# Attention and a gated feed-forward on one Trainium2 core: q loads on GpSimd's queue, a norm in small pieces, products and sums moved in chunk 1

## The chip, the cores and the metric

The kernel runs on one core of a Trainium2 chip. The core has five engines with instruction streams of their own: TensorE (PE in the profile; PEld is its loading of weights), VectorE (DVE), ScalarE (ACT), GpSimd (POOL) and SyncE (SP), which here only issues DMA transfers. ACT and GpSimd can issue transfers too. Every engine executes its stream in order and waits on semaphores for the others. The metric is the time of one execution on the device, in microseconds (us).

## What is computed

The reference, cut to what matters. The attention has no softmax, so k and v are first contracted to a 64 x 64 matrix for each head; every row of a head's output is normalised by its root mean square. The result, 4608 rows of 512, goes through a gated feed-forward layer. The weights come in 64-bit floats.

```python
# q, k, v: (8 batches, 8 heads, 576, 64)   w_gate, w_val: (512, 1536)   w_out: (1536, 512)
kv  = einsum('bhsd,bhse->bhde', k, v)
out = einsum('bhsd,bhde->bhse', q, kv)
rms = sqrt(mean(out * out, axis=-1, keepdims=True) + 1e-06)
x   = (out / rms * g_norm).transpose(0, 2, 1, 3).reshape(8 * 576, 512)
gate = 1 / (1 + exp(-(x @ w_gate)))
y    = (gate * (x @ w_val)) @ w_out
```

## The kernel before

**Chunks.** The feed-forward works in nine chunks of 512 rows. Chunk 0 is computed plainly (`Plain`, L592; `second`, L828). Chunks 1 to 8 use a fast scheme of matrix multiplication: sums of blocks of x, of the weights and of h are formed first, so that 26 block products do the work of 32 (`PRODUCTS1` for the first layer, `PRODUCTS2` for the second; `X_SUMS`, `SUMS` and `W_SUMS` list the sums). The first layer of a chunk, `first_layer_fast`, runs three blocks j = 0, 1, 2 of 26 products, so 78 places p = 0 to 77, about 0.86 us of PE each (L952). The second layer, `second_layer_fast`, runs 26 products over the three blocks (L1056).

**Attention beside it.** Batch 0 is done at the start (`attention`). The attention of batch b = 1 to 7 is cut into steps (`feed`) that are put between the matmuls of chunk b - 1, at places written out by hand: `places` for chunk 0, where a place is a matmul of 512 columns and runs from 0 to 87, and `where` for the later chunks, where it is p. A batch has two head runs, m = 0 and 1. The steps of one run are: two turns of q by VectorE (t, L402 and L404), the matmuls into a PSUM tile of three banks called `at` (u, L433), the square by ACT (q in `where`, L438), two sums by VectorE (s, L441), the root by ACT (r, L444), the norm (n) and two transposes back by VectorE with their stores to the x ring (x, L456 to L467). There is one `at` tile, so the second run's matmuls, and the next batch's key-value products (L387, L394), wait until the norm of the run before has read it. In batches 1 and 2 the norm is a reciprocal on VectorE (L477, L479) and 18 scalings by ACT (L473), one for every head slice; in the later batches VectorE does it.

**Loads.** `load_q_run(b, m)` brings a run's q in transposed order: 12 transfers, eight of 32 x 18 pieces of 128 bytes (L118) and four of 32 x 2 pieces (L119). All are issued by SP (`nc.sync`), in program order with the 24 + 12 halves of the weight units (`load_unit`, L160 and L162) and with k and v of the coming batch (`load_late`, L133 and L138). Batch 1's q goes into space of h that is not in use yet. A weight unit is 512 rows by 128 columns of w_gate and of w_val, converted from 64-bit words by five VectorE and two ACT instructions (`convert`: L196, L211, L223, L227, L234 on VectorE, L201 and L216 on ACT). Three units are staged at a time; the next load of a stage waits for VectorE's L227 of the unit that was in it.

**Fast products.** After product i of the first layer `combine` executes its steps: copies out of PSUM by ACT (L918), sums by VectorE (L922), sigmoids by ACT (L911), and products of the gate and the value (the steps with `*`, L914) by the engine that is given as `mult`. Five PSUM banks go round: a product that opens a region takes the bank that was freed longest ago, and `give_all` frees a region's bank after its last step. In a block's last product (K, i = 25) the regions H and K are open; the sums `o6=H+t8` and `o4=o4+K` release their banks. The products of h then feed the sums of h (`h_sums`, L726), which GpSimd makes, except eight that VectorE makes in the third block. GpSimd executes a block's sums one for each later product.

**Sums of weights.** The sums of w_gate and w_val are made once by GpSimd (`w1_sums`, L745), during chunk 0 and the start of chunk 1. The sums of w_out (`w_form`, L1027 and L1029) are made once, in chunk 1, at places listed for the first layer (`at1`) and the second (`at2`), each on GpSimd or on VectorE, as the third number says; each is stored to a scratch in device memory, from which later chunks load it.

Of the kernel before, what the change touches and what calls it, by code (L numbers as in the profile page):

```python
# [20 lines left out]
def kernel(  # L21
# [11 lines left out]
    nc = tc.nc  # L33

    B, H, S, HD = q.shape
# [69 lines left out]
    def load_q_run(b, m):  # L105
        if b >= B:
            return
        if b == 1:
            t = h_main[2 - m].rearrange("p s c -> p (s c)")[:, 4 * NT * P - QW:4 * NT * P]
        else:  # L110
            t = sb.tile([P, QW], FP32, tag="q", name="q", bufs=1)
        main = t[:, 0:2 * S].rearrange("p (e j c) -> p e j c", e=2, c=QB)
        more = t[:, 2 * S:QW].rearrange("p (e j c) -> p e j c", e=2, c=QB)
        for i in range(NC):
            for e in range(2):
                for g in range(2):
                    src = q[b, 4 * m + 2 * g + e].rearrange("(p j) d -> p j d", j=JR)[:, :, QB * i:QB * i + QB]
                    nc.sync.dma_start(out=main[HD * g + QB * i:HD * g + QB * i + QB, e], in_=src)  # L118
                nc.sync.dma_start(out=more[QB * i:QB * i + QB, e], in_=src[:, JR - 2:JR])  # L119
        q_late[b, m] = t  # L120

    kv_late = {}
# [251 lines left out]
    def feed(b):  # L374
# [35 lines left out]
        def heads_run(m):  # L410
# [57 lines left out]
                                                          in_=xTs[p0:p0 + QB, i, :, s0:s0 + n_])  # L468
                            s0 += n_

            def norm(r):
                for n in range(6 * r, 6 * r + 6):
                    nc.scalar.activation(out=by_head(sq)[:, n], in_=by_head(d["u"])[:, n], func=AF.Copy,  # L473
                                         scale=ms[:, n:n + 1])
# [12 lines left out]
        u0, u1 = heads_run(0), heads_run(1)  # L487
        if b == 1:
            return kv, t0 + t1 + u0 + u1, ()
        names = "t00 t01 t10 t11 u0 q0 s00 s01 r0 n00 n01 x00 x01 u1 q1 s10 s11 r1 n10 n11".split()  # L490
        steps_ = dict(zip(names, t0 + t1 + u0 + u1[:7]))
# [7 lines left out]
        return kv, first, u1[7:]  # L499

    def flush():
        while fill:
# [129 lines left out]
    for token in order.split():  # L632
# [13 lines left out]
        else:  # L646
            a[f][steps[name]]()
            if token == f"Q{NE - 1}":
# [29 lines left out]
    PRODUCTS2 = (("A", 8, 4, "o5=A"), ("C", 9, 1, "o4=C"), ("B", 18, 10, "o3=B"), ("A", 24, 14, "o1=A"),  # L678
# [253 lines left out]
    def first_layer_fast(c, at):  # L932
# [3 lines left out]
        for j in range(N3):  # L936
            o = {f"t{n}": pair(temps[:, i]) for i, n in enumerate((0, 1, 8, 9))}
            for n in (3, 1, 2, 0):
                o[f"o{n}"] = pair(sg_tile())
            h = h_main[j].rearrange("p (g e t) c -> p g e (t c)", g=2, e=2)  # L940
            for n in range(4):
                o[f"o{4 + n}"] = h[:, :, n // 2, GH * (n % 2):GH * (n % 2) + GH]
            regions = {}
            for i, (name, hv, wv, steps) in enumerate(PRODUCTS1):
                part, p = next(n for n, r in enumerate(PARTS) if i in r), NPR * j + i
                new = name not in regions
                if new:
                    i_ = free.popleft()
                    regions[name] = i_, pair(bank(i_))
                ws = w1_form(c, j, part, hv)  # L950
                for g in range(2):
                    nc.tensor.matmul(regions[name][1][:, g], ws[:, g], xf[c][wv], start=(new and g == 0), stop=True,  # L952
                                     skip_group_check=True)
                combine(o, regions, steps, nc.vector if i == NPR - 1 and (j == N3 - 1 or c == 1 and j == 1) else nc.gpsimd)
                give_all(regions, LAST1, i)
                for step in at.get(p, ()):
                    step()
                for _ in range(2 if i % HALF == HALF - 1 else 1):
                    if h_fill:
                        h_fill.popleft()[1]()  # L960
                if c > 1:
                    g_ = NPA * (N3 * (c - 2) + j) + part
                    if p < NPR * N3 - 1:
                        wait = (3 if part < 2 else 0) if j == 0 and c + 1 < B else 0
                        if wait and i == PARTS[part][-1]:
                            held[i + wait] = g_ + NPA
                        elif i == PARTS[part][-1]:
                            load_granule(g_ + NPA)
                        if j == 0 and i in held:
                            load_granule(held.pop(i))  # L970
                    if stores and p >= 24 and p % 2 == 0:
                        stores.popleft()()
                    k_, r = divmod(p - (38 if c == 2 else 20), 2)
                    if r == 0 and 0 <= k_ < NR:
                        load_w((c - 2) * NS + k_)
                else:
                    if p == 0:
# [151 lines left out]
    for c in range(1, NG):  # L1129
# [15 lines left out]
                else:  # L1145
                    x_late.append((p - NPR, step))
        if c == 1:
            for at_, forms in ((at1, ((28, 9, 0), (30, 10, 0), (34, 12, 0), (52, 8, 1), (56, 13, 0), (58, 14, 0), (64, 16, 1), (66, 11, 1), (74, 19, 0))), (at2, ((1, 22, 0), (3, 23, 1), (4, 25, 1), (9, 15, 0), (10, 24, 0), (10, 20, 0), (11, 17, 0), (12, 18, 0), (13, 21, 0)))):
                for p, n, pool_ in forms:
                    at_.setdefault(p, []).append(lambda n=n, eng=nc.gpsimd if pool_ else nc.vector, at_once=at_ is at1: w_form(n, eng, at_once))  # L1150
        first_layer_fast(c, at1)
        if c == 1:
            sgs += [spare_sg] + more_sgs
# [31 lines left out]
```

## Time and profile before

| what | value |
|---|---|
| time, median of 3 runs | 1014.05 us (1013.87 to 1014.34) |
| the profiled execution, its own time | 1011.93 us |
| its span, first to last instruction | 1010.2 us |
| mean granted TensorE clock | 0.998 |
| PE busy | 996.6 us, 99% |
| DVE busy | 720.6 us, 71% |
| POOL busy | 587.5 us, 58% |
| ACT busy | 341.7 us, 34% |
| transfers | 195.42 MB, mean 193 GB/s |

Three chunks in the chain of work that ended last, all by lines of PE: chunk 0 plain up to 162.72 us, chunk 1 from there to 270.92, and chunk 2 to 377.74. A chunk from the second to the sixth takes 106.6 us, of which 5.0 belong to the attention of the next batch; the last two, which have none beside them, take 101.0.

How to read it: all times are from the start of the span. "Busy" leaves out register, branch, semaphore and DMA-issuing instructions. Matmuls are pipelined and their ends are modelled, so PE's share of 99% hides stalls of some tenths of a microsecond; they are seen as gaps between the starts of matmuls. In the waits, "A <- B" means that engine A's instruction waited, and that B was what came last. SPq and POOLq stand for the instruction queues that issue transfers.

### The profile page before, as it was taken

The page shows a single profiled execution, that of the slowest core. Times are in us where ns is not written, and L with a number is a line of the kernel's source. Part 1 is how long each engine was busy: PE and PEld are TensorE (multiplying, and loading weights), DVE is VectorE, ACT ScalarE, POOL GpSimd, SP SyncE. Part 2 cuts the span into 40 slices and gives each one's busy share as a digit, 9 for nine tenths or more (in the row PEclk, how much of TensorE's full clock was granted, in tenths as well). Part 3 has the DMA queues.
Part 4 walks back from the last instruction along what each step waited for, and adds up shares of the span by engine and source line. Part 5 has one row for each costly group of instructions (what it writes and reads, how often), then busy time and mean ns, then how long its engine had stood idle before and what let it go on. Part 6 is the DMA issues. An engine that isn't in the chain of part 4 may idle for free.

```text
span 1010.2 us, 16595 instructions
## 1 busy us (share of the span) xinstructions
PE 996.6 (99%) x5958; PEld 819.5 (81%) x5958; DVE 720.6 (71%) x1201; ACT 341.7 (34%) x605; POOL 587.5 (58%) x961
## 2 busy tenths in 40 slices
PE   8999999999999999999999999999999999999998
PEld 7444446878888888888888888888888888888887
DVE  4968998889768847775667666866688556755672
ACT  4547432472134303441244114421352133213320
POOL 0000899896539651967187706962596449744963
PEclk9999999999999999999999999999999999999999
DMA  9887423664699569756776477756764545444514
GB/s 274 241 230 222 153 81 97 217 201 163 198 306 278 166 202 274 222 161 200 224 240 197 151 231 237 218 158 183 247 208 151 174 157 210 163 150 159 213 57 123
DMA packets 165201, 195.42 MB, mean 193 GB/s; under 512 B 94560, under 2 KB 138208, under 8 KB 165120
## 3 DMA queue, kind: packets, MB, share of 16 engines
q0 software_dynamic: 20976, 112.87, 32.7%
q1 hardware_dynamic: 136976, 79.40, 28.3%
q10 hardware_dynamic: 7168, 2.10, 0.9%
q8 instruction: 47, 0.77, 0.3%
q14 instruction: 34, 0.28, 0.1%
HBM read 160.50 MB, written 25.56 MB: 184 GB/s over the span
## 4 chain that ended last, share of the span: by engine, by line
PE 89%; SPq 3%; DVE 3%; DMA 3%; ACT 2%; issue 1%; POOL 0%; ACTq 0%; DVEq 0%; POOLq 0%
PE mm L952 52%; PE mm L1056 26%; PE mm L828 4%; SPq L118 2%; PE mm L592 2%; PE at L433 1%; DMA st<-in_moe_w_val_dram 1%; PE at L387 1%; SPq L119 1%; ACT sqs L473 1%; PE at L592 1%; DMA h_more<-in_v_dram 1%; DMA h_more<-in_k_dram 1%; PE mm L645 0%; DVE w L1029 0%
## 5 line engine op out<-in xcount | busy, mean ns | idle before, releaser
L952 PE MATMUL mm<-xs,w 128*128 128x256 f32 x1428 | 332.2, 380 | 0.6 <-DVE h L922 0.5
L952 PEld LDWEIGHTS mm<-xs,w 128*128 128x128 f32 x1428 | 271.1, 191 | 37.5 <-DVE h L922 0.9
L952 PE MATMUL mm<-xT,w 128*128 128x256 f32 x948 | 230.1, 380 | 0.5 <-ACT temps L918 0.5
L952 PEld LDWEIGHTS mm<-xT,w 128*128 128x128 f32 x948 | 180.0, 191 | 25.3 <-ACT temps L918 0.9
L922 DVE TENSOR_TENSOR sg<-sg,mm 128x512 f32<-128x512 f32 (+1 forms) x176 | 100.9, 600 | 86.6 <-PE mm L952 41.8
L774 POOL DMA_DIRECT2D w<-kept x84 | 46.9, 558 | 191.3 <-PE mm L952 189.0
L1056 PE MATMUL mm<-w,h 128*128 128x256 f32 x630 | 142.9, 380 | 0.0
L1056 PEld LDWEIGHTS mm<-w,h 128*128 128x128 f32 x630 | 120.0, 191 | 16.1 <-POOL h L726 0.2
L918 ACT COPY temps<-mm 128x512 f32<-128x512 f32 (+1 forms) x128 | 66.2, 539 | 188.1 <-PE mm L1056 94.7
L726 POOL TENSOR_TENSOR h<-h 128x128 f32<-128x128 f32 x216 | 113.3, 536 | 16.7 <-DVE h_more L726 13.2
L914 POOL TENSOR_TENSOR h<-h,sg 128x512 f32<-128x512 f32 x69 | 91.9, 1348 | 50.0 <-DVE h L922 30.0
L1056 PE MATMUL mm<-w,h_more 128*128 128x256 f32 x474 | 108.5, 380 | 0.7 <-DVE h L922 0.7
L911 ACT ACTIVATE sg<-sg 128x512 f32<-128x512 f32 x96 | 59.7, 630 | 134.5 <-DVE sg L922 134.5
L1056 PEld LDWEIGHTS mm<-w,h_more 128*128 128x128 f32 x474 | 90.3, 191 | 13.0 <-DVE h L922 1.1
L918 ACT COPY sg<-mm 128x512 f32<-128x512 f32 (+1 forms) x112 | 57.1, 511 | 87.4 <-PE mm L1056 48.1
L726 POOL TENSOR_TENSOR h_more<-h 128x128 f32<-128x128 f32 x120 | 62.6, 525 | 36.5 <-DVE h L914 32.2
L592 PE MATMUL mm<-xT,w 128*128 128x512 f32 x176 | 78.8, 602 | 0.9 <-DVE w L234 0.8
L922 DVE TENSOR_TENSOR temps<-temps,mm 128x512 f32<-128x512 f32 (+1 forms) x96 | 59.5, 620 | 26.5 <-PE mm L1056 17.2
L922 DVE TENSOR_TENSOR temps<-mm,temps 128x512 f32<-128x512 f32 (+1 forms) x64 | 39.8, 622 | 53.7 <-PE mm L1056 23.6
L918 ACT COPY h<-mm 128x512 f32<-128x512 f32 x48 | 28.2, 588 | 138.3 <-PE mm L952 124.8
L922 DVE TENSOR_TENSOR sg<-mm,sg 128x512 f32<-128x512 f32 (+1 forms) x64 | 39.7, 620 | 44.2 <-PE mm L952 23.5
L745 POOL TENSOR_TENSOR h_more<-w 128x256 f32<-128x256 f32 x10 | 10.6, 1074 | 101.9 <-DMA st<-in_moe_w_out_dram 101.9
(140 smaller groups left out, 1278.8 us busy)
## 6 DMA issues: line engine op xcount, KB each, us to landing
w<-kept POOLq DMA_DIRECT2D x42, 896.0 KB, 5.2
w<-kept POOLq DMA_DIRECT2D x90, 384.0 KB, 4.6
w<-kept POOLq DMA_DIRECT2D x42, 768.0 KB, 5.2
out_dram<-sg SPq DMA_DIRECT2D x119, 64.0 KB, 1.7
h_more<-in_k_dram SPq DMA_DIRECT2D x28, 256.0 KB, 5.3
h_more<-in_v_dram SPq DMA_DIRECT2D x28, 256.0 KB, 5.6
q<-in_q_dram SPq DMA_DIRECT2D x96, 72.0 KB, 5.1
xT<-xTs SPq DMA_DIRECT2D x96, 72.0 KB, 4.5
```

What stands on the lines that cost most here:

```text
L118: nc.sync.dma_start(out=main[HD * g + QB * i:HD * g + QB * i + QB, e], in_=src)
L592: nc.tensor.matmul(self.ps[i], w[("wg", "wv")[i], self.f][:, m, :], xT[self.c][:, m, :], start=(m == 0), stop=(m == NMT - 1), skip_group_c ...
L726: ops.append((eng, lambda v=v, x=x, sign=sign, y=y, eng=eng: eng.tensor_tensor(out=h_form(v, j), in0=h_form(x, j), in1=h_form(y, j), op=op ...
L745: nc.gpsimd.tensor_tensor(out=w1_slot(j, w_at[v]), in0=w1_slot(j, w_at[x]), in1=w1_slot(j, w_at[y]), op=op_of(sign))
L774: nc.gpsimd.dma_start(out=granule(g)[:, 0:n], in_=kept1[g // NPA % N3, g % NPA][:, 0:n])
L828: nc.tensor.matmul(ps[t], gv[0, f][:, P * t:P * t + P], w["wo", f], start=(f == 0), stop=(f == NFT - 1), skip_group_check=True)
L911: nc.scalar.activation(out=o["o" + step[1]], in_=o["o" + step[1]], func=AF.Sigmoid)
L914: mult.tensor_tensor(out=o[x], in0=o[x], in1=o[y], op=ALU.mult)
L918: nc.scalar.copy(out=o[out_], in_=o[expr])
L922: tt(out=o[out_], in0=o[x], in1=o[y], op=ALU.add if sign == "+" else ALU.subtract)
L952: nc.tensor.matmul(regions[name][1][:, g], ws[:, g], xf[c][wv], start=(new and g == 0), stop=True, skip_group_check=True)
L1056: nc.tensor.matmul(regions[name][1], h_form(hv, j), ws[:, j], start=(used[i] and j == 0), stop=(j == N3 - 1), skip_group_check=True)
```

## The change

Four edits.

1. `load_q_run` takes its queue by the batch: batch 1's 24 transfers are issued by GpSimd (`nc.gpsimd`), all others by SP as before. In the program they stand at places 2 and 11 of chunk 0, ahead of GpSimd's first sums of the weights (place 73).
2. Batch 2's norm, in chunk 1, was the reciprocal with six scalings, then twelve more; now it is the reciprocal as a step of its own and six steps of three scalings. The hand-written places are new: the first run's root moves from 42 to 35, its norm from 48 and 50 to 36 to 44, its transposes from 52 and 53 to 51 and 52; the second run's norm from 60 and 62 to 62 to 69.
3. In chunk 1's second block (j = 1) the three products of K's group go from VectorE to GpSimd. In all chunks and blocks the steps of that group are in a new order: the sum and the product of o7 first.
4. Form 13 of w_out, a sum on VectorE, moves from place 56 of chunk 1's first layer to the second finished product of its second layer; form 22 moves one product further there. Form 13 is still stored at once.

```diff
-                    nc.sync.dma_start(out=main[HD * g + QB * i:HD * g + QB * i + QB, e], in_=src)
-                nc.sync.dma_start(out=more[QB * i:QB * i + QB, e], in_=src[:, JR - 2:JR])
+        queue = nc.gpsimd if b == 1 else nc.sync
+                    queue.dma_start(out=main[HD * g + QB * i:HD * g + QB * i + QB, e], in_=src)
+                queue.dma_start(out=more[QB * i:QB * i + QB, e], in_=src[:, JR - 2:JR])
...
-            def norm(r):
-                for n in range(6 * r, 6 * r + 6):
+            def norm(r, per=6):
+                for n in range(per * r, per * r + per):
...
-                norms = [lambda: (nc.vector.reciprocal(ms, ms), norm(0)), lambda: (norm(1), norm(2))]
+                norms = [lambda: nc.vector.reciprocal(ms, ms)] + [lambda r=r: norm(r, 3) for r in range(6)]
...
-        where = """0:t00 5:t01 25:u0 26:q0 28:t10 30:s00,s01 33:t11 42:r0 48:n00 50:n01 52:x00 53:x01,u1
-                   56:q1 57:s10,s11 60:r1,n10 62:n11""" if b == 2 else """
+        where = """0:t00 5:t01 25:u0 26:q0 28:t10 30:s00,s01 33:t11 35:r0 36:n00 37:n01 39:n02 40:n03 42:n04 43:n05 44:n06
+                   51:x00 52:x01 53:u1 56:q1 57:s10,s11 60:r1 62:n10,n11 63:n12 65:n13 66:n14 68:n15 69:n16""" if b == 2 else """
...
-                 ("K", 43, 2, "o4=o4+K o7=o7-t8 o4*o0 o6=H+t8 o6*o2 o7*o3"))
+                 ("K", 43, 2, "o7=o7-t8 o7*o3 o4=o4+K o4*o0 o6=H+t8 o6*o2"))
...
-                combine(o, regions, steps, nc.vector if i == NPR - 1 and (j == N3 - 1 or c == 1 and j == 1) else nc.gpsimd)
+                combine(o, regions, steps, nc.vector if j == N3 - 1 and i == NPR - 1 else nc.gpsimd)
...
-            at1: (52, 8, 1), (56, 13, 0), (58, 14, 0) ...     at2: (1, 22, 0), (3, 23, 1) ...
+            at1: (52, 8, 1), (58, 14, 0) ...                  at2: (1, 13, 0), (2, 22, 0), (3, 23, 1) ...
-            at_once=at_ is at1
+            at_once=at_ is at1 or n == 13
```

More of the change, by code (lines that the diff above doesn't have):

```diff
@@ L489, in feed @@
             return kv, t0 + t1 + u0 + u1, ()
-        names = "t00 t01 t10 t11 u0 q0 s00 s01 r0 n00 n01 x00 x01 u1 q1 s10 s11 r1 n10 n11".split()
-        steps_ = dict(zip(names, t0 + t1 + u0 + u1[:7]))
-        where = """0:t00 5:t01 25:u0 26:q0 28:t10 30:s00,s01 33:t11 42:r0 48:n00 50:n01 52:x00 53:x01,u1
-                   56:q1 57:s10,s11 60:r1,n10 62:n11""" if b == 2 else """
+        n_ = "n{0}0 n{0}1 n{0}2 n{0}3 n{0}4 n{0}5 n{0}6" if b == 2 else "n{0}0 n{0}1"
+        names = f"t00 t01 t10 t11 u0 q0 s00 s01 r0 {n_.format(0)} x00 x01 u1 q1 s10 s11 r1 {n_.format(1)}".split()
+        steps_ = dict(zip(names, t0 + t1 + u0 + u1[:-2]))
+        where = """0:t00 5:t01 25:u0 26:q0 28:t10 30:s00,s01 33:t11 35:r0 36:n00 37:n01 39:n02 40:n03 42:n04 43:n05 44:n06
+                   51:x00 52:x01 53:u1 56:q1 57:s10,s11 60:r1 62:n10,n11 63:n12 65:n13 66:n14 68:n15 69:n16""" if b == 2 else """
                    5:t00 8:t01 28:u0 29:t10 30:q0 33:s00,s01 36:r0 39:t11 41:n00 47:n01 51:x00,x01 54:u1
@@ L498, in feed @@
         first = [(int(w_.split(":")[0]), steps_[x]) for w_ in where.split() for x in w_.split(":")[1].split(",")]
-        return kv, first, u1[7:]
+        return kv, first, u1[-2:]
     def flush():
@@ L1147 @@
         if c == 1:
-            for at_, forms in ((at1, ((28, 9, 0), (30, 10, 0), (34, 12, 0), (52, 8, 1), (56, 13, 0), (58, 14, 0), (64, 16, 1), (66, 11, 1), (74, 19, 0))), (at2, ((1, 22, 0), (3, 23, 1), (4, 25, 1), (9, 15, 0), (10, 24, 0), (10, 20, 0), (11, 17, 0), (12, 18, 0), (13, 21, 0)))):
+            for at_, forms in ((at1, ((28, 9, 0), (30, 10, 0), (34, 12, 0), (52, 8, 1), (58, 14, 0), (64, 16, 1), (66, 11, 1), (74, 19, 0))), (at2, ((1, 13, 0), (2, 22, 0), (3, 23, 1), (4, 25, 1), (9, 15, 0), (10, 24, 0), (10, 20, 0), (11, 17, 0), (12, 18, 0), (13, 21, 0)))):
                 for p, n, pool_ in forms:
-                    at_.setdefault(p, []).append(lambda n=n, eng=nc.gpsimd if pool_ else nc.vector, at_once=at_ is at1: w_form(n, eng, at_once))
+                    at_.setdefault(p, []).append(lambda n=n, eng=nc.gpsimd if pool_ else nc.vector, at_once=at_ is at1 or n == 13: w_form(n, eng, at_once))
         first_layer_fast(c, at1)
```

## The prediction

> **What bounds the kernel now.** I read, in this order: the page's shares, the waits of PE, the chain of waits that ended last, busy time by stretches, then the timelines around every stall. PE is busy 99% of the span, so only a stall of PE, or work that keeps PE waiting, is worth anything. The waits of PE (what waited, for what: us in total, times, longest) name the long ones:
>
> ```profile
> PE at L433 <- ACT sqs L473: 3.2, 2, 2.5
> PE mm L592 <- DVE w L234: 0.8, 1, 0.8
> ```
>
> The 2.5 us is one stall of chunk 0 at 75.7 us: the second head run of batch 1 needs the PSUM tile that the norm of the first (ACT, L473) still reads. The chain of waits (start, length, what) says why that norm is late:
>
> ```profile
> 53.48 1.38 SPq L118
> ...
> 58.19 4.41 DMA st<-in_moe_w_val_dram
> 62.62 0.70 DVE w L196
> ...
> 98.75 3.67 ACT sqs L473 x18
> ```
>
> SP issues batch 1's q in small pieces (L118) up to 58.2; only then can it issue the second half of weight unit 6, for which VectorE waits. The stretches (us, then busy time of PE, PEld, DVE, ACT, POOL, clock, DMA share, GB/s):
>
> ```profile
> 55.00:60.00 5.00, 5.00 (x13) 2.10 (x11) 0.81 (x2) 0.00 (x0) 0.00 (x0) 1.00 0.53 85
> 75.00:77.50 2.50, 0.73 (x2) 0.00 (x0) 0.48 (x2) 2.50 (x10) 0.00 (x0) 1.00 1.05 354
> 77.50:80.00 2.50, 1.73 (x68) 1.73 (x70) 2.46 (x3) 2.47 (x6) 0.00 (x0) 0.71 0.73 135
> 80.00:82.50 2.50, 2.50 (x15) 1.33 (x10) 2.50 (x7) 0.38 (x2) 0.00 (x0) 0.61 0.43 67
> 209.00:230.60 21.60, 19.54 (x152) 15.75 (x151) 18.58 (x26) 14.69 (x43) 20.95 (x29) 1.00 0.63 210
> ```
>
> While SP issues q, the transfers run at 85 GB/s where 354 is seen elsewhere, and VectorE idles: the issuing queue is the limit, not the DMA engines. After PE's long stall the granted clock is 0.71 and 0.61 for two stretches. The last line is chunk 1: PE idles while GpSimd is full. A quiet chunk, the seventh, gives the yardstick:
>
> ```profile
> 804.27 67.34 PE mm L952 x312
> ```
>
> Chunk 1's first layer runs from 162.72 to 236.11 (PE's timeline), 73.39 us, where 67.34 and two head runs of 1.31 make 69.96: 3.4 us are lost, all between 209 and 231. Its second layer takes 34.81 against 33.67: 1.1 us are lost. From chunk 2 on nothing is.
>
> **The q loads of batch 1, on GpSimd's queue.** They leave SP's queue (24 issues, 30.8 to 38.8 and 48.9 to 58.2) and go ahead of all GpSimd work, which starts at 103.27. What GpSimd's first issue must wait for is PE's last transpose of the first batch (21.6), so they start near 21.7, not 30.8. Price of an issue, from GpSimd's timeline, which has no 128-byte pieces:
>
> ```profile
> 309.76 0.76 POOL L1012 DMA_DIRECT2D w<-kept  x1
> 311.35 0.55 POOL L1012 DMA_DIRECT2D w<-kept  x1
> ```
>
> The first has 384 pieces (three in each of 128 partitions), the second 128: 0.21 us for 256 more. Sixteen q issues have 576 pieces, eight have 64: 0.92 and 0.50 by that slope, 0.55 the lower bound, and 576/128 of 0.55, 2.5 us, the upper. I take the slope, since two rows carry it: 16 x 0.92 + 8 x 0.50 = 18.7 us, all issued by about 41 and landed by 46 (5.1 us, the median of such loads). VectorE takes the first run at 48.2 and the second at 66.8, so both are hidden; at 2.5 us the second would land at 71, late by 4.
>
> On SP the weight halves move up: unit 6's second half from 58.2 to about 45, behind batch 1's k and v. VectorE then goes on at 55.4 instead of 62.6, 7 us earlier, so unit 6 is ready at 64 where PE wants it at 70.3, and the norm's last scaling, 78.3 now, ends near 71 where PE wants its PSUM at 74.8. What goes: 0.8 (L592), 2.5 (L433), the lost clock (0.29 + 0.39) x 2.5 = 1.7, and the 0.4 for which batch 2's key-value products wait on the second run's norm, the last chain line above: 5.4 us. Bounds: 0 (q late) to 6 with the restarts of PE. Nothing later holds the gain back by the rows: GpSimd's first sum (L745) starts 0.8 us after those products start, so it comes forward with PE.
>
> A sentence apart on a rule: the Trainium skill's SBUF — State Buffer, section "Who interferes with whom", says that a DMA from GpSimd's queue has its descriptors written by GpSimd, which VectorE locks out while it runs a two-port operation such as tensor_scalar, and that whoever comes first keeps the port for its whole instruction. It speaks against this edit; it would lengthen the issues by some share of the eight conversions of that kind in 23 to 44 us, and no row here shows a DMA issue beside one. At 0.69 each, eight of them put the last landing at 51.5, which changes nothing.
>
> **Batch 2's norm.** The same 36 ACT scalings (0.2 us apart), in twelve groups of three; for the first run the root goes from place 42 to 35 and the groups to 37-44, done before the second run at place 53 needs the PSUM tile. In the second run copies of PSUM come between groups. The same two table loads stay. This removes the stalls at 211 (0.64 waiting for ACT), 216.5 (0.33) and 223 (0.49), all behind ACT. The work is hidden under PE; the two x transposes move one place up on VectorE.
>
> **Products and w_out sum in chunk 1.** VectorE loses three products (0.94, 0.69, 0.95) and, until the second layer, form 13 (2.26): 4.8 us at its fullest place, so the stall at 229.5 (0.51 waiting for DVE) goes too. All 3.4 us can go. In the second layer form 13 costs VectorE 1.2 to 2.3 behind the h sums; form 24, next in need, has 1.6 us of slack and VectorE arrives about 1.5 earlier: nothing. GpSimd pays:
>
> ```profile
> 208.69 1.28 POOL L914 TENSOR_TENSOR h<-h,sg 128x512 f32<-128x512 f32 x1
> 226.96 1.81 POOL L1027 TENSOR_TENSOR w<-w 128x768 f32<-128x768 f32 x1
> 227.19 2.13 DVE L922 TENSOR_TENSOR sg<-sg,temps 128x512 f32<-128x512 f32 x1
> 234.20 1.28 POOL L914 TENSOR_TENSOR h<-h,sg 128x512 f32<-128x512 f32 x1 [3.63 <-ACT sg L911]
> ```
>
> From 208.69 to 230.6 it waits for nobody; three more products are 3.84. Four h sums beside VectorE's products took 0.9 instead of 0.45, so up to 2 come back. It reaches the product o5 (the last row) at 232.4 to 234.4 on the old clock and ends it at 233.7 to 235.7. PE, 3.4 us ahead, wants it as the third block of the second layer: 236.11 + 0.86 - 3.4 = 233.6. So 0.1 to 2.1 us late; I take 0.8, nearer the low end, because VectorE leaves GpSimd alone there. The 1.1 us of the second layer stays: one operation more before H's release, but VectorE 0.6 or more ahead. Chunk 1: -3.4 + 0.8 = -2.6; bounds -4 and +0.8 (rival C).
>
> **The new order in K's group**, in every chunk. In the third block VectorE makes the products. Chunk 2:
>
> ```profile
> 343.25 0.69 DVE L922 TENSOR_TENSOR temps<-temps,mm 128x512 f32<-128x512 f32 x1 [0.17 <-PE mm L952]
> 344.11 0.69 DVE L922 TENSOR_TENSOR h<-h,mm 128x512 f32<-128x512 f32 x1 [0.18 <-PE mm L952]
> 344.71 0.68 DVE L922 TENSOR_TENSOR h<-h,temps 128x512 f32<-128x512 f32 x1
> 345.31 0.69 DVE L914 TENSOR_TENSOR h<-h,sg 128x512 f32<-128x512 f32 x1
> 345.92 0.69 DVE L922 TENSOR_TENSOR h<-mm,temps 128x512 f32<-128x512 f32 x1
> ```
>
> The last one frees H's bank, which the second layer's fourth product takes; it ends at 346.61, and PE takes the bank 3.02 us after that layer's start (343.91), at 346.93. New order: o7 can start at 343.85, K's sum third, H's fifth, 0.6 apart: 346.25 to 346.94. PE loses about 0.07 and 0.1 for its restart, 0.17 in each of seven chunks: +1.2; bounds 0 and 2.5 (0.35 each).
>
> **Sum.** -5.4 - 2.6 + 1.2 = -6.8 us on a span of 1010.2; that execution took 1011.93, the median is 1014.05, 0.2% more: 1014.05 - 6.8 = 1007.2.
>
> **Rivals.**
> A, slower: every VectorE operation that uses the port, not only a few, keeps GpSimd from writing its pieces. VectorE is busy 23.2 of 25 us between 25 and 50, so GpSimd gets 7% of the 26.5 us up to 48.2, 1.9 us of the 9.4 that the first run needs; VectorE then waits for the other 7.5 and a landing, 12.6 us, and for the second run again, some 8.5 + 5.1. That is 26 us for the 7 of idle time that it has now, and PE waits with it: 1014.05 + 19 - 2.6 + 1.2 = 1031.7. It decides from where GpSimd gets less than 18.7 of the 40 us up to 61.7, a landing ahead of 66.8. For: the 2.13 row, a VectorE operation of 0.69 behind GpSimd's 1.81. Against: there both read operands; and an issue of 0.58 at 349.8 in chunk 2 stood beside VectorE sums of two operands.
> B, no change: VectorE pays for the port. Eight conversions (L196, L211, from 23.7 to 43.3) held 0.92 each are 7.4 us, the idle time that was to be won; unit 1's, at 23.7 and 25.3, push PE's second tile by up to 1.2. 1014.05 + 1.2 - 2.6 + 1.2 = 1013.9. Issues of 2.5 us, landed only at 71, end near it: 1012.7. For: these operations do 1024 elements in 0.69, twice the pace of L223's 1.22, so they use the port otherwise than the sums do. Against: VectorE has short waits of its own there (0.4 us behind the one at 25.3) that would take part of it. The rule of the Trainium skill cited above gives this case if GpSimd comes first.
> C: chunk 1 turns from ACT and DVE to GpSimd. At 1.98 a product (the dearest of this chunk, at 188.9) o5 ends at 230.6 + 5.9 + 1.3 = 237.8, 4.2 late: chunk 1 -3.4 + 4.2, sum -5.4 + 0.8 + 1.2 = -3.4, 1010.7. For: GpSimd is idle for 1.0 of the 39.6 us from 191 to 230.6. Against: it is idle for 3.63 behind them.
> D: chunk 0's gain is not carried on. Between 121.5 and 162.7 DVE is busy 40.64 and POOL 40.34 of 41.2 us; if either starts its share no earlier, the 5.4 are returned: 1014.05 - 2.6 + 1.2 = 1012.7. Against: both start behind PE or behind VectorE's conversions, which come forward.
>
> **How the numbers follow.** Forecast 0.64, A 0.08, B 0.08, C 0.14, D 0.06. The forecast's own range is 1004.3 to 1009.8: -9.7, near the sum of the best ends, to -4.3, with 1 us less from each of the first two parts and half a microsecond more at H's bank. The range 1004.3 to 1012.8 also takes in C and D and leaves out A, B and a little of the rest. 0.2% (2 us) is about what a measurement of this kernel can tell from no change: faster is the forecast, C and half of D, 0.81; same is B and the other half, 0.09 with what B may lose beyond; slower, A and the dear end of B, 0.10.
>
> **What would show it.** Right: GpSimd's q issues between 21.7 and 45 at 0.9 us, no VectorE gap near 55 to 62, no PE wait for L473 in chunk 0, clock 1.00 there, chunk 1's first layer near 70 us, a PE wait of 0.2 or less 3 us into each second layer. Wrong: VectorE waiting at L402 for q (A), conversions (L196, L211) over 1 us (B), PE waiting for GpSimd's L914 at chunk 1's second layer (C), chunk 0 shorter but chunk 1 longer (D).

## The result

| | before | changed |
|---|---|---|
| median of 8 executions | 1014.19 us (1012.30 to 1015.92) | 1010.61 us (1009.16 to 1011.98) |
| ratio, 95% interval | | 0.9965 (0.9954 to 0.9976) |
| the profiled execution: time, span | 1011.93, 1010.2 us | 1010.92, 1009.1 us |

The kernel became 3.6 us faster, about half of the 6.8 that were forecast, and is 3.4 us short of the predicted time. 1010.61 lies outside the forecast's own range (1004.3 to 1009.8); it is inside the whole range (to 1012.8) only because that also took in rivals C and D, neither of which happened. The two spans differ by 1.1 us only: the profiled execution of before was 2.3 us faster than the median of its kernel, that of the changed kernel 0.3 slower. So the stages are read one by one, from PE's first product of each layer to that of the next (us):

| stage | before | changed | difference | predicted |
|---|---|---|---|---|
| ahead of chunk 0 | 21.63 | 21.61 | 0 | 0 |
| chunk 0 | 140.96 | 135.77 | -5.19 | -5.4 |
| chunk 1, first layer | 73.56 | 70.46 | -3.10 | -3.4 |
| chunk 1, second layer | 34.65 | 35.85 | +1.20 | +0.8 |
| chunks 2 to 8, first layers | 499.67 | 501.47 | +1.80 | 0 |
| chunks 2 to 8, second layers | 235.47 | 239.75 | +4.28 | +1.2 |

The first three rows are near the forecast, and chunk 1's second layer is 0.4 over it. The last row is not near: every second layer of chunks 2 to 8 takes 0.61 us longer, where 0.17 was forecast. The row above it holds 1.25 us in chunk 4, where PE waits for a load of v, and 0.55 in chunk 2, told at the end. The waits of PE in the changed kernel (what waited, for what: us in total, times, longest), from the view of waits:

```profile
PE mm L1058 <- DVE h L924: 3.2, 8, 0.8
...
PE at L388 <- ACT sqs L474: 1.0, 1, 1.0
PE at L388 <- DMA h_more<-in_v_dram: 0.9, 1, 0.9
...
PE mm L954 <- DVE temps L924: 0.5, 1, 0.5
PE mm L1058 <- POOL h L916: 0.4, 1, 0.4
```

The 3.2 us for the norm at the head runs and the 0.8 for unit 6 are gone. In their place PE's products of the second layer (L1058) wait eight times, once in each of chunks 1 to 8, for a sum of VectorE (L924). The wait view leaves out PE's restart, so its sums are below the losses of the table. The second row is batch 2's key-value products, which were to lose their 0.4 and now wait 1.0 for the norm of batch 1's second run.

The stretches show chunk 0's gain (us, then busy time of PE, PEld, DVE, ACT, POOL, clock, DMA share, GB/s); the last line is chunk 1 from 203.80, the 21.6 us that answer to 209.00 of before:

```profile
55.00:60.00 5.00, 5.00 (x32) 2.09 (x34) 4.39 (x6) 2.19 (x2) 0.00 (x0) 1.00 0.94 270
75.00:77.50 2.50, 2.50 (x30) 1.38 (x22) 2.50 (x7) 0.38 (x1) 0.00 (x0) 1.00 0.44 69
77.50:80.00 2.50, 2.50 (x7) 1.14 (x6) 1.88 (x3) 2.50 (x4) 0.00 (x0) 1.00 0.96 310
80.00:82.50 2.50, 2.50 (x7) 1.09 (x6) 2.41 (x4) 0.81 (x1) 0.00 (x0) 1.00 0.96 296
203.80:225.40 21.60, 21.60 (x166) 18.69 (x165) 17.59 (x26) 13.62 (x33) 21.05 (x29) 1.00 0.61 199
```

VectorE, idle for 4.2 of the 5 us from 55 before, is busy for 4.4 of them; the transfers run at 270 GB/s instead of 85; PE's 2.5 us stall and the two stretches at clocks of 0.71 and 0.61 are gone. In chunk 1 PE is busy for all 21.6 us, against 19.54, with GpSimd as full as before.

### The profile page after: what moved, and what is told of

Same layout as the page of the kernel before. It is cut to its first block, busy times and chain, and to the rows that moved or that the text cites. A ratio compares the mean times of both kernels' runs of the same rounds, so it can differ in the third digit from the quotient of the medians.

```text
span 1009.1 us, 16638 instructions
## 1 busy us (share of the span) xinstructions
PE 995.6 (99%) x5958; PEld 815.0 (81%) x5958; DVE 720.5 (71%) x1198; ACT 341.9 (34%) x605; POOL 602.0 (60%) x988
## 4 chain that ended last, share of the span: by engine, by line
PE 70%; DVE 4%; DMA 1%; POOL 1%; issue 0%; DVEq 0%; POOLq 0%
PE mm L954 45%; PE mm L1058 22%; DVE h L924 2%; PE at L434 1%; DMA h_more<-in_v_dram 1%; DVE h L916 1%; PE at L388 1%; POOL h L728 1%; DVE temps L924 1%; POOL h_more L728 0%; PE at L395 0%; DMA xT<-xTs 0%; POOL w_ring L1029 0%; DVE w L1029 0%; DVE w L1031 0%
## 5 line engine op out<-in xcount | busy, mean ns | idle before, releaser
L954 PEld LDWEIGHTS mm<-xT,w 128*128 128x128 f32 x948 | 179.5, 190 | 25.2 <-issue 0.5
L924 DVE TENSOR_TENSOR sg<-sg,mm 128x512 f32<-128x512 f32 (+1 forms) x176 | 100.8, 600 | 93.5 <-PE mm L954 43.2
L1058 PE MATMUL mm<-w,h 128*128 128x256 f32 x630 | 143.4, 379 | 0.5 <-POOL h L916 0.4
L1058 PEld LDWEIGHTS mm<-w,h 128*128 128x128 f32 x630 | 119.5, 190 | 17.5 <-POOL h L916 0.8
L1058 PE MATMUL mm<-w,h_more 128*128 128x256 f32 x474 | 109.9, 381 | 2.9 <-DVE h L924 2.9
L1058 PEld LDWEIGHTS mm<-w,h_more 128*128 128x128 f32 x474 | 89.5, 190 | 17.6 <-DVE h L924 5.7
L924 DVE TENSOR_TENSOR temps<-temps,mm 128x512 f32<-128x512 f32 (+1 forms) x96 | 59.4, 619 | 26.8 <-PE mm L1058 17.4
L924 DVE TENSOR_TENSOR temps<-mm,temps 128x512 f32<-128x512 f32 (+1 forms) x64 | 39.8, 622 | 49.7 <-PE mm L1058 23.3
L924 DVE TENSOR_TENSOR sg<-mm,sg 128x512 f32<-128x512 f32 (+1 forms) x64 | 39.6, 619 | 45.1 <-PE mm L954 23.6
L594 PEld LDWEIGHTS mm<-xT,w 128*128 128x128 f32 x176 | 32.6, 190 | 39.2 <-issue 36.4
```

The lines of the kernel that those rows point to most:

```text
L594: nc.tensor.matmul(self.ps[i], w[("wg", "wv")[i], self.f][:, m, :], xT[self.c][:, m, :], start=(m == 0), stop=(m == NMT - 1), skip_group_c ...
L924: tt(out=o[out_], in0=o[x], in1=o[y], op=ALU.add if sign == "+" else ALU.subtract)
L1058: nc.tensor.matmul(regions[name][1], h_form(hv, j), ws[:, j], start=(used[i] and j == 0), stop=(j == N3 - 1), skip_group_check=True)
```

## Where the second layers lose it

VectorE in chunk 2's third block, from its timeline (start, length, engine, line, operation; in brackets idle time before it):

```profile
336.69 0.69 DVE L924 TENSOR_TENSOR temps<-temps,mm 128x512 f32<-128x512 f32 x1 [0.17 <-PE mm L954]
337.42 0.69 DVE L924 TENSOR_TENSOR h<-h,temps 128x512 f32<-128x512 f32 x1
338.21 0.69 DVE L916 TENSOR_TENSOR h<-h,sg 128x512 f32<-128x512 f32 x1
338.82 0.68 DVE L924 TENSOR_TENSOR h<-h,mm 128x512 f32<-128x512 f32 x1
339.53 0.69 DVE L916 TENSOR_TENSOR h<-h,sg 128x512 f32<-128x512 f32 x1
340.14 0.68 DVE L924 TENSOR_TENSOR h<-mm,temps 128x512 f32<-128x512 f32 x1
```

And PE beside it:

```profile
337.36 2.32 PE L1058 MATMUL mm<-w,h 128*128 128x256 f32 x10
339.51 1.03 PE L1058 MATMUL mm<-w,h_more 128*128 128x256 f32 x4
340.88 1.35 PE L1058 MATMUL mm<-w,h_more 128*128 128x256 f32 x5 [0.34 <-DVE h L924]
```

The steps are t8, o7's sum, o7's product, o4's sum, o4's product, and H's sum, which frees the bank. Their starts are 0.73, 0.79, 0.61, 0.71 and 0.61 us apart. Where a step reads the result of the one just ahead (o7's sum reads t8, each product reads the sum before it) it is 0.71 to 0.79; where it doesn't, 0.61. The view puts no idle time in brackets for them: the pause is hidden in the spacing, since independent operations start 0.61 us apart though each lasts 0.69. H's sum starts 2.78 us after the second layer's first product and ends at 340.82; PE wants the bank 3.02 after that product, at 340.38, and takes it at 340.88. That is 0.50 late; the next matmul is 0.61 late, and so is the rest of the layer.

In the kernel before the same sum started 2.01 us after the layer's first product. There each of o7's sum, o4's product and H's sum stands behind a step that it does not read, and H's sum ended 0.32 us before PE took the bank.

## The experiments

All times are ratios to the kernel before, measured on the same chip as the run, with 95% intervals (the runs were on more than one chip); stages are of one profiled execution each. Single executions of one kernel differ by up to some 8 us, so stages carry the readings and the ratios confirm them. (In microseconds: 0.001 is 1.)

| kernel | ratio | chunk 0 | chunk 1, first | chunk 1, second | second layers 2 to 8 |
|---|---|---|---|---|---|
| before | 1 | 140.96 | 73.56 | 34.65 | 235.47 |
| changed | 0.9965 (0.9954 to 0.9976) | 135.77 | 70.46 | 35.85 | 239.75 |
| q edit alone | 0.9933 (0.9915 to 0.9952) | 136.64 | 73.55 | 34.26 | 235.47 |
| new order alone | 1.0050 (1.0031 to 1.0070) | 140.53 | 73.06 | 35.64 | 239.75 |
| chunk 1's edits, old order | 0.9974 (0.9960 to 0.9988) | 141.37 | 71.22 | 34.81 | 235.47 |
| changed, old order | 0.9925 (0.9906 to 0.9943) | 135.27 | 71.20 | 34.94 | 235.48 |
| changed, pairs split | 0.9937 (0.9918 to 0.9956) | 135.28 | 70.45 | 35.52 | 237.50 |
| changed, H's sum first | 0.9929 (0.9910 to 0.9948) | 134.98 | 71.09 | 35.19 | 236.46 |
| norm alone | 0.9978 (0.9963 to 0.9993) | 141.12 | 72.05 | 34.75 | 235.47 |
| H's sum first, o5 on VectorE | 0.9931 (0.9913 to 0.9949) | 135.08 | 72.39 | 35.08 | 236.44 |
| changed, order by block | 0.9919 (0.9894 to 0.9944) | 134.94 | 70.49 | 35.02 | 235.48 |

**The q edit alone**, on the kernel before:

```diff
+        queue = nc.gpsimd if b == 1 else nc.sync
-                    nc.sync.dma_start(out=main[HD * g + QB * i:HD * g + QB * i + QB, e], in_=src)
-                nc.sync.dma_start(out=more[QB * i:QB * i + QB, e], in_=src[:, JR - 2:JR])
+                    queue.dma_start(out=main[HD * g + QB * i:HD * g + QB * i + QB, e], in_=src)
+                queue.dma_start(out=more[QB * i:QB * i + QB, e], in_=src[:, JR - 2:JR])
```

> The kernel before with the q edit alone. Theory S (SP's issuing of small pieces delays unit 6 and the norm, as predicted): chunk 0 ends as early as in the changed kernel, chunk 1 starting at about 157.4 us instead of 162.6, no wait for unit 6 and none of 2.5 us at the second head run; second layers of chunks 2 to 8 at 33.67 us as before; the time falls by 5 us, ratio near 0.995. Rival G (the gain of chunk 0 needs the other edits, or chunk 1, whose stalls stand behind VectorE and GpSimd, gives it back): chunk 0 short but chunk 1 longer by 3 to 5 us, time within 1.5 us of before.

Chunk 1 started at 158.24, chunk 0 was 4.3 us shorter, and chunk 1 gave nothing back: theory S, and against rival D of the prediction too. Later only chunk 6 grew, by 0.97 us, where PE waits for a load of v. Chunk 0's gain is 0.9 us less than in the changed kernel: 0.4 of it is lost at 23.8 us, in batch 0's attention, and 0.4 at batch 2's key-value products, which wait 1.4 for the norm here and 1.0 there. By the ratios this one edit does more (0.9933) than the whole change (0.9965).

**The new order alone**, on the kernel before:

```diff
-                 ("K", 43, 2, "o4=o4+K o7=o7-t8 o4*o0 o6=H+t8 o6*o2 o7*o3"))
+                 ("K", 43, 2, "o7=o7-t8 o7*o3 o4=o4+K o4*o0 o6=H+t8 o6*o2"))
```

> The kernel before with the new order of K's group alone. Theory D (on VectorE a sum or product that reads the result of the instruction just ahead starts 0.7 to 0.8 us after it instead of 0.6, and the new order makes four such steps in a row): each second layer of chunks 2 to 8 takes 34.28 us instead of 33.67, 7 x 0.61 = 4.3 us more, about 1018.3 in all, ratio 1.004. Rival P (the prediction's: five operations 0.6 apart): 0.17 in each of seven, 1.2 us more, ratio 1.001, second layers at 33.85.

Second layers of 34.28, 4.28 us in all, and a ratio of 1.0050: against rival P, and as theory D has it. Theory D's 34.28 was read from the changed kernel, so this run shows that the order alone makes the loss, not yet by which mechanism; that is left to the run with the pairs split. (Three of the steps, not four, read the one just ahead: o7's sum and the two products.) The waits of PE name one cause:

```profile
PE mm L1056 <- DVE h L922: 4.1, 8, 1.7
```

The longest, 1.7, is chunk 1's, where VectorE comes later still (0.7 before). In chunk 1's first layer the order saves half a microsecond, which nobody had expected.

**Chunk 1's edits with the old order**: the changed kernel with this, and q on SP:

```diff
-                 ("K", 43, 2, "o7=o7-t8 o7*o3 o4=o4+K o4*o0 o6=H+t8 o6*o2"))
+                 ("K", 43, 2, "o4=o4+K o7=o7-t8 o4*o0 o6=H+t8 o6*o2 o7*o3"))
-        queue = nc.gpsimd if b == 1 else nc.sync
+        queue = nc.sync
```

> The kernel before with the norm in small pieces, the products of chunk 1's second block on GpSimd and the moved w_out sums; q on SP and K's group in the old order. Theory D: chunk 1's first layer falls from 73.56 to about 70.5 us, and its second layer from 34.65 to 33.7 to 34.6, since the old order frees H's bank in time (what is left is 0.6 for GpSimd's late o5); the time falls by 3 to 4 us, ratio 0.9965. Prediction's: first layer 70.2, second 35.4 (the 1.1 at H's bank stays, 0.8 for o5 is new), -2.6 us, ratio 0.9975. Chunk 0 as before (chunk 1 starts at 162.6).

The second layer did not go down: 34.81, against 34.65 before and theory D's 33.7 to 34.6. But what it waits for is another: the wait at H's bank is gone and PE waits 0.5 for GpSimd's o5 and, later, for a sum of h. So the 1.1 us that the prediction let stay go once VectorE is relieved of the products and form 13, if the order is the old one. The first layer stopped at 71.22, short of both expectations (70.5 and 70.2): one stall is left, up to 218.0, where PE waits for ACT and loses 0.58 us. ACT's timeline in this kernel, and then in the changed one:

```profile
215.66 0.59 ACT L920 COPY sg<-mm 128x512 f32<-128x512 f32 x1
217.36 0.58 ACT L920 COPY sg<-mm 128x512 f32<-128x512 f32 x1 [1.10 <-POOL h L916]
```

```profile
209.55 1.08 ACT L920 COPY sg<-mm 128x512 f32<-128x512 f32 x2
```

ACT copies the next block's regions into tiles of sg that GpSimd's products of the block before still read. With the old order the second copy waits 1.10 us for them; with the new one, whose first product is o7*o3, both copies follow at once. That is what the new order is worth, in the blocks where GpSimd multiplies; the last run below tests it.

**The changed kernel with the old order** (the first of the two hunks above):

> The changed kernel with K's group back in the old order. Theory D: second layers of chunks 2 to 8 at 33.67 us (-4.3 against the changed kernel's 34.28) and chunk 1's second layer down from 35.85 to about 34.8, since its 1.1 us at H's bank comes from the same order: 1010.6 - 5.3 = 1005.3 us, ratio 0.9915. Rival O (the order is there for GpSimd, whose first product the new order brings forward; undoing it holds up the sums of h): chunk 1's second layer longer than 35.85 by 0.5 us or more, and the gain under 3.5 us, 1007 or above.

Second layers at 33.67 and chunk 1's second layer at 34.94, as theory D has it; chunk 1's first layer lost the 0.74 us again. Rival O was wrong in its place (the second layer) but right that the order serves GpSimd's products. The ratio, 0.9925, is 1 us short of the 0.9915 expected, which lies inside its interval. In the profiled execution, 1007.11 us, chunk 0 began 2.1 us later, PE waiting 1.6 us for batch 0's first q; four of the six executions lie between 1006.97 and 1007.37, two at 1004.65 and 1004.81. Whether the four all had that wait is not shown. VectorE in chunk 2:

```profile
337.98 0.69 DVE L924 TENSOR_TENSOR temps<-temps,mm 128x512 f32<-128x512 f32 x1 [0.17 <-PE mm L954]
338.85 0.69 DVE L924 TENSOR_TENSOR h<-h,mm 128x512 f32<-128x512 f32 x1 [0.17 <-PE mm L954]
339.45 0.68 DVE L924 TENSOR_TENSOR h<-h,temps 128x512 f32<-128x512 f32 x1
340.05 0.69 DVE L916 TENSOR_TENSOR h<-h,sg 128x512 f32<-128x512 f32 x1
340.65 0.68 DVE L924 TENSOR_TENSOR h<-mm,temps 128x512 f32<-128x512 f32 x1
```

Four steps, none of which reads the one ahead of it, 0.60 apart: H's sum starts 2.67 us after that of t8, not 3.45.

**Pairs split**, on the changed kernel:

```diff
-                 ("K", 43, 2, "o7=o7-t8 o7*o3 o4=o4+K o4*o0 o6=H+t8 o6*o2"))
+                 ("K", 43, 2, "o7=o7-t8 o4=o4+K o7*o3 o4*o0 o6=H+t8 o6*o2"))
```

> The changed kernel with H's sum still fifth of the six steps, but no step right behind the one whose result it reads (both sums first, then two products, then H's sum). Theory D (four steps in a row that read the one before cost 0.12 to 0.20 us each on top of 0.6): H's sum starts 3.16 us after the sum of t8 instead of 3.45, so second layers of chunks 2 to 8 at 33.99 us instead of 34.28, chunk 1's wait at H's bank 0.8 instead of 1.1: 2.3 us less than the changed kernel. Rival Q (only the place in the queue counts, not what a step reads): 34.28 as in the changed kernel, no difference.

Second layers of 33.96 (33.99 expected), 237.50 in all; chunk 1's 35.52. H's sum is fifth as in the changed kernel, and swapping two steps took 2.25 us out of seven layers, so rival Q is out: what a step reads counts, not its place alone. Nor are products slow as such: behind a step that they don't read they start 0.60 after it. By this, of the 4.28 us, 2.25 are the two products right behind their own sums. The other 2.03 are the place, fifth instead of fourth, and o7's sum, which still stands right behind the sum of t8 that it reads; no run parts these two.

**H's sum first**, on the changed kernel:

```diff
-                 ("K", 43, 2, "o7=o7-t8 o7*o3 o4=o4+K o4*o0 o6=H+t8 o6*o2"))
+                 ("K", 43, 2, "o6=H+t8 o7=o7-t8 o4=o4+K o7*o3 o4*o0 o6*o2"))
```

> The changed kernel with H's sum first of the six steps, the products in the new order. Theory D: H's bank comes free 0.7 us after the sum of t8, long before PE wants it: second layers of chunks 2 to 8 at 33.67 us, chunk 1's down from 35.85 to about 34.7, and, since the products keep the new order, chunk 1's first layer at 70.5 (with the old order it was 71.2): 5.4 us less than the changed kernel, 1005.2, body (from chunk 0's first product on) 1.2 shorter than with the old order. Rival R (the delay goes on to the next in the row: K's bank or the sums of h, which come later by a step): second layers of 33.9 or more.

Half a miss. H's bank is free in time, yet the second layers are 33.81, not 33.67: 0.14 us each are left, as rival R says in kind (33.9 was its number). In chunk 1 the view of waits names what is late next, a sum of h on GpSimd (0.2). In the later chunks it lists nothing so short, but the timelines show the same: in chunks 2 and 3 PE falls back at 341.12 and 447.90, 0.05 us after GpSimd's second sum of h ends (341.07 and 447.85). And chunk 1's first layer is 71.09, not 70.5, though the products keep their order. VectorE there:

```profile
210.94 0.69 DVE L924 TENSOR_TENSOR sg<-sg,mm 128x512 f32<-128x512 f32 x1 [0.46 <-PE mm L954]
211.55 2.55 DVE L1031 SCALAR_TENSOR_TENSOR w<-w,w 128x768 f32<-128x768 f32 x1
```

A sum of w_out (1.23 us in the next block, at 226.41 of the changed kernel) takes 2.55 here; in the changed kernel the same one took 1.93. GpSimd was at a sum of its own of 1.82 from 211.46. PE then waits 0.5 for VectorE.

**The norm alone**: the kernel before with only the hunks of batch 2's norm and its places:

```diff
...
-                norms = [lambda: (nc.vector.reciprocal(ms, ms), norm(0)), lambda: (norm(1), norm(2))]
+                norms = [lambda: nc.vector.reciprocal(ms, ms)] + [lambda r=r: norm(r, 3) for r in range(6)]
...
```

> The kernel before with batch 2's norm in small pieces alone. Theory N (the stalls at 210.5 and 222.8 stand behind ACT's long norm, those at 216 and 229 behind the products): chunk 1's first layer falls from 73.56 to about 72 us, the other part of the fall to 71.2 needs the products; 1.5 us less, ratio 0.9985. Rival M (VectorE, which has the three products and form 13, is what holds chunk 1; a shorter wait for ACT changes nothing): 73 us or more.

72.05: theory N. Chunk 1's 3.10 us are then 1.5 by the norm (73.56 to 72.05), 0.8 by the moved products and form (to 71.22) and 0.8 by the new order (to 70.46), when they are added in this sequence; alone on the kernel before, the new order gave 0.5.

**o5's product on VectorE** in chunk 1's third block, on the kernel with H's sum first:

```diff
-                combine(o, regions, steps, nc.vector if j == N3 - 1 and i == NPR - 1 else nc.gpsimd)
+                combine(o, regions, steps, nc.vector if j == N3 - 1 and (i == NPR - 1 or c == 1 and i == 20) else nc.gpsimd)
```

> As with H's sum first, and in chunk 1's third block the product o5*o1 made by VectorE instead of GpSimd. Theory L (PE's 0.6 us wait at the third product of chunk 1's second layer is GpSimd coming late to o5 behind its sums): that wait goes, chunk 1's second layer 0.6 shorter than with H's sum first alone. Rival V (VectorE is as full there: it pays 0.7 and the sum of t8 and H's come late instead): no difference or longer.

The wait for o5 went, as theory L says, and was paid more than twice over: chunk 1's first layer is 1.3 us longer, with a wait of 1.0 for GpSimd's sums of h, and in the second the wait for the next of these is 0.7 instead of 0.2. Rival V has the outcome, no gain; neither theory named the place. The ratio shows no difference.

**Order by block**: the changed kernel, with the old order where VectorE multiplies:

```diff
+                if j == N3 - 1 and i == NPR - 1:
+                    steps = "o4=o4+K o7=o7-t8 o4*o0 o6=H+t8 o6*o2 o7*o3"
                 combine(o, regions, steps, nc.vector if j == N3 - 1 and i == NPR - 1 else nc.gpsimd)
```

> The changed kernel with the new order of K's group in the first two blocks, where GpSimd makes the products, and the old one in the third, where VectorE makes them. Theory D: second layers of chunks 2 to 8 at 33.67 us, chunk 1's first layer at 70.5 as in the changed kernel (new order: 70.46 and 70.45; old order: 71.20 and 71.22), its second at 34.9; chunk 0 at 135 to 135.8: from chunk 0's first product on 976.3 us where the old order everywhere has 976.94 and the changed kernel 983.30, about 1004.5 to 1006 in all. Rival B (the 0.7 us of chunk 1's first layer come from another place than the first two blocks' order): first layer 71.2, no better than the old order everywhere.

First layer 70.49, second layers 33.67: both halves of theory D. In its profiled execution the part from chunk 0's first product on is 978.62 us and not 976.3, as PE waited for loads of v twice:

```profile
PE at L388 <- DMA h_more<-in_v_dram: 1.8, 2, 1.4
...
PE mm L954 <- DVE temps L924: 0.5, 1, 0.5
```

The two waits for v cost 2.4 us with PE's restarts, 1.69 in chunk 2 and 0.73 in chunk 4. The median is 1005.92 us, ratio 0.9919, the lowest of all kernels run. Its interval ends at 0.9944, below that of the changed kernel (from 0.9954); it overlaps those of the q edit alone and of the other orders that undo the loss, so it is not shown to be better than these.

## Why the prediction was right, and where it was off

**The q loads: the cause right, the size in part by luck.** The term was 5.4, and chunk 0 became 5.19 shorter. GpSimd's first and last issues in the changed kernel (timeline):

```profile
22.05 1.51 POOL L119 DMA_DIRECT2D h<-in_q_dram  x2 [20.74 <-DMA st<-in_moe_w_val_dram]
...
30.07 0.55 POOL L120 DMA_DIRECT2D h<-in_q_dram  x1 [2.59 <-DMA h<-in_q_dram]
...
37.09 0.97 POOL L120 DMA_DIRECT2D h<-in_q_dram  x1 [1.23 <-DMA h<-in_q_dram]
...
41.24 0.55 POOL L120 DMA_DIRECT2D h<-in_q_dram  x1
```

Start at 22.05 (21.7 was forecast), end at 41.8 (41), by two errors that cancel, which is luck: an issue of 576 pieces cost mostly 0.67 us (0.92 was taken by the slope), and GpSimd stood 3.8 us behind its own earlier loads, eight of which were under way at a time.

The prediction added up PE's stalls: 0.8, 2.5, 1.7 of lost clock and the 0.4 at batch 2's key-value products. But these products wait for the norm of batch 1's second run, before and after the change, and that wait takes back what PE gains or loses ahead of it. In the run of chunk 1's edits with the old order, which has q on SP and the same 2.5 us stall, the granted clock stays at 1.00 behind the stall (stretches, as above):

```profile
77.50:80.00 2.50, 0.74 (x48) 0.74 (x52) 1.95 (x2) 2.48 (x8) 0.00 (x0) 1.00 1.06 261
80.00:82.50 2.50, 2.50 (x44) 1.48 (x34) 2.50 (x6) 1.11 (x2) 0.00 (x0) 1.00 0.54 84
```

Chunk 0 is no shorter there: it takes 141.37, and the products wait 1.9 for the norm instead of 0.4. That norm follows the first run's at a fixed distance. ACT's last scalings of the first run and all of the second, in the kernel before and then in that run:

```profile
76.81 1.41 ACT L473 ACTIVATE sqs<-at,ms 128x64 f32<-128x64 f32 x6
98.66 3.76 ACT L473 ACTIVATE sqs<-at,ms 128x64 f32<-128x64 f32 x18
```

```profile
77.80 1.41 ACT L474 ACTIVATE sqs<-at,ms 128x64 f32<-128x64 f32 x6
99.55 3.77 ACT L474 ACTIVATE sqs<-at,ms 128x64 f32<-128x64 f32 x18
```

From the end of the first norm (78.22 and 79.21) to the start of the second it is 20.43 and 20.34 us. In all eleven profiled kernels it is 20.33 to 20.52, the three with a lowered clock behind the stall having 20.43 or more, the others 20.37 or less; and chunk 1 starts 60.1 us after the products in each. So chunk 0's gain is the advance of the first norm, and the lowered clock is worth 0.1 to 0.2 us, not 1.7. In the changed kernel the first norm ended at 73.09, 5.1 us earlier, where the prediction had it "near 71", 7 earlier. The products' wait grew to 1.0 where 0.4 was to vanish, since PE came earlier by more than the norm. A loss of 0.48 at 50.9, for a load of v, went too and had not been counted. That SP's issuing held up unit 6, and unit 6 the norm, is right; that the sum of the stalls came so near is luck. Why the norm came 2 us later than forecast, and what sets the 20.3 us behind it, was not tried.

**Rivals A and B: no.** VectorE did not starve GpSimd. The port is felt, though: the first four conversions took 0.78 to 0.86 instead of 0.69, the later ones 0.69, and the issue at 37.09, of 64 pieces, 0.97 instead of 0.55 beside a conversion. The Trainium skill's "SBUF — State Buffer", section "Who interferes with whom", has an exclusive port which goes to whoever issued first; these rows agree in kind. The sum of it here, 0.5 us of VectorE's time, is far below the idle time that it had.

**Batch 2's norm and the products: right in kind**, -3.10 for -3.4. PE's timeline has no gap left in that layer, so 70.46 is the layer without stalls, and the yardstick of 69.96 was 0.5 too low. The edits that the term was about gave 2.3 of it (71.22 with the old order); the other 0.8 came from the new order, which the prediction had not counted here. GpSimd's late o5 cost 0.67 for 0.8, so rival C (4.2 late) fell, though its sign, PE waiting for that product, is there. Rival D fell as well: chunk 1 starts 5.2 us earlier and loses none of it.

**The new order of K's group: the step that failed.** The prediction put "K's sum third, H's fifth, 0.6 apart", so that H's sum would end 0.01 us after PE wanted the bank, and 0.17 us a chunk, with "bounds 0 and 2.5 (0.35 each)". Measured: 0.61 a chunk, 4.28 in all, above the bound. The spacing of 0.60 was read from the four rows of the old order, in which no step reads the one ahead. The profile of before held the other price at two places in the same block, three sums in a chain, 0.79 and 0.72 apart, and the product behind H's sum of 345.92, 0.79 apart:

```profile
331.23 0.69 DVE L922 TENSOR_TENSOR temps<-mm,temps 128x512 f32<-128x512 f32 x1 [1.01 <-PE mm L952]
332.02 0.69 DVE L922 TENSOR_TENSOR temps<-temps,mm 128x512 f32<-128x512 f32 x1
332.74 0.92 DVE L922 TENSOR_TENSOR h<-h,temps 128x512 f32<-128x512 f32 x1
...
346.71 1.52 DVE L914 TENSOR_TENSOR h<-h,sg 128x512 f32<-128x512 f32 x2
```

With 0.73, 0.79, 0.61, 0.71 and 0.61 for the five spacings H's sum starts 0.45 later than with five of 0.60; PE, whose slack was nil, comes 0.50 late and loses 0.1 more at its restart.

**Chunk 1's second layer**: the 1.1 us at H's bank was said to stay "one operation more before H's release, but VectorE 0.6 or more ahead". It stayed (0.92 before, 1.11 now, with the restart), but only because the new order put back what the moved work had given: with the old order it is gone. The forecast also left out a third loss there, 0.39 us at 254.1, where PE waits for a sum of h on GpSimd.

**Sum.** -5.4 - 2.6 + 1.2 = -6.8 was forecast; the same terms measured are -5.2 - 1.9 + 4.3 = -2.8. With chunk 2's 0.55 and chunk 4's 1.25 that is -1.0, as the two spans have it. The medians moved by 3.6, with an interval from 2.4 to 4.7. Some of what lies between is waits that come and go: loads of v (0.7 to 1.7 us with PE's restart, in chunk 2, 4 or 6 of five of the eleven profiled executions, at most 0.35 in the others) and of batch 0's q. Why they come when they do was not tried, so this rest stays open. 3.6 is near rival C's 3.4, by other causes: that is chance.

## What to carry over

Before putting steps of one engine in a new order, sort them into those that read the result just ahead and those that don't, and price the two apart from rows of the profile; a producer and its consumer want a third step between them. An order that is good for one engine (GpSimd's products free a tile earlier) can be bad for another that runs the same list, so give each its own. And where PE has no slack at a bank, an error in the assumed spacing of the steps is paid in full, in every chunk. Last, stalls ahead of a common wait don't add up: look for the wait that ends last, and forecast by how much its releaser comes earlier.

## What was not expected of the hardware

VectorE's spacing: 128x512 operations of 0.68 to 0.69 us follow each other at 0.60 when independent, and at 0.71 to 0.79 when the second reads the first's result. The Trainium skill's "Perfetto Trace Analysis", section "Optimizing Scalar/DVE Operations", says that the part of an instruction's profiled time in which its writes are acknowledged overlaps with the next instruction. The 0.60 agree; the dependent ones start after the profiled end.

VectorE and GpSimd on sums of two operands in SBUF: in chunk 2 of the changed kernel, VectorE and then GpSimd:

```profile
324.73 0.69 DVE L924 TENSOR_TENSOR temps<-temps,mm 128x512 f32<-128x512 f32 x1
325.46 1.74 DVE L924 TENSOR_TENSOR h<-h,temps 128x512 f32<-128x512 f32 x1
```

```profile
325.36 0.47 POOL L728 TENSOR_TENSOR h_more<-h,h_more 128x128 f32<-128x128 f32 x1
325.78 0.46 POOL L728 TENSOR_TENSOR h_more<-h_more,h 128x128 f32<-128x128 f32 x1
326.19 0.45 POOL L728 TENSOR_TENSOR h_more<-h_more 128x128 f32<-128x128 f32 x1
326.60 0.91 POOL L728 TENSOR_TENSOR h<-h 128x128 f32<-128x128 f32 x1
```

The sum that reads PSUM takes 0.69; the next, with both operands in SBUF, 1.74, over three of GpSimd's sums, and GpSimd's fourth then takes twice its time. How long VectorE's sum takes goes by which of GpSimd's three small sums it starts beside, in the traces of all eleven kernels, and what PE loses at that place in chunk 2 goes by how long it takes:

| VectorE's sum starts beside | kernels | it takes | PE loses |
|---|---|---|---|
| the third | before, q edit alone, norm alone | 0.90 to 0.92 | 0 |
| the second | four (chunk 1's edits with the old order, old order, H's sum first, o5 on VectorE) | 1.27 to 1.31 | 0.26 to 0.31 |
| the second | new order alone | 0.95 | 0 |
| the first | changed, pairs split, order by block | 1.74 to 1.79 | 0.74 to 0.78 |

In the new order alone VectorE came between, and GpSimd's third sum took 0.90 instead of 0.45; why is open. So a shift of tenths in one engine's order can cost or save that much far from the edit. It makes chunk 2's 0.55 in the table of the result: 0.74 lost here in the changed kernel, against 0.19 lost to a load of v before.
